# First convolution product of a conformer block: 13 of 16 chunks as two seven-product quads inside the attention passes

## The chip, the cores and the metric

The kernel runs on one core of a Trainium2 chip. The metric is the device time of one execution in microseconds; the times given are medians of several executions. The kernel before has a median of 1873.56 us over 3 runs (1873.33 to 1876.11).

The engines are TensorE (PE in the profile; PEld is its weight load), VectorE (DVE), ScalarE (ACT), GpSimd (POOL) and SyncE (SP), which issues nearly all of the DMAs. TensorE writes to eight PSUM banks, called s0 to s3 and y0 to y3 in the profile (numbers left out: s and y), and numbered 0 to 7 in the code.

## The reference, cut to what matters

A conformer block for 2 sequences of 4000 tokens with 512 features, in bfloat16: half a feed-forward step, attention with one head, a convolution module, another half feed-forward step. The change touches the convolution module's first product, `h @ w_pw1`, with its gate:

```
    x2 = x1 + attn
    h = _layernorm(x2, axis=-1)
    h = h @ w_pw1                      # 512 x 1024
    a = h[..., :D].copy()
    b = h[..., D:].copy()
    h = a * _sigmoid(b)
    ...                                # 3 taps over time, then a normalization over all tokens
    h = _silu(dc) @ w_pw2
    x3 = x2 + h
```

Each token's 512 normalized features give 1024 columns; the first 512 (values) are multiplied by the sigmoid of the last 512 (gates).

## The kernel before

**Chunks and stages.** The 8000 tokens are 16 chunks of 512 (`NCK`), eight to a sequence (`TCB`); the last chunk of a sequence, 7 and 15, has 416 tokens. The program has three stages: the first feed-forward step over all chunks, then 16 attention passes (one for each chunk of queries, `attention`), then the rest of the convolution module and the second feed-forward step.

**A pass.** Pass `g` goes over 32 key tiles (`KT`) in steps `kt` = 0 to 31. In passes 0 and 8 (`plain`), scores are computed tile by tile. In the others they are computed in seven-product quads (`score_quad`): a 2 x 2 block product with 7 block products instead of 8, at the price of sums of blocks on both sides. A quad holds three banks: c, x and h. Products 1 and 2 go to c; product 5 goes to x and is copied aside; ScalarE copies c's first product into h, to which products 6, 7 and 4 are added in turn, with VectorE reading h between them (`plus`). The softmax-weighted values are computed in the same way by pairs of tiles (`pv`, seven products over banks 3 to 6 and 7). The last value products, left-over tiles and row sums of pass `g` are done in steps 0 to 6 of pass `g + 1` (`units_late`); the new pass's value products begin in step 7 (`units`). In between, steps 0 to 6 hold the late products of the pass before, and its output is projected in steps 9 and 13 and normalized for the convolution in steps 9 to 20 (`ln_beside`), by ScalarE, with DMA transposes into `lnT[0]`.

**The convolution's first product.** `pw1` computes one block of 128 output columns with four matmuls of 512 columns. `conv_b` does a gate block and its tanh; `conv_a` does a value block and multiplies it by one plus the tanh (the factor of a half is in the taps' weights). The hook of the passes (`att_hook`) calls `pair(t, jj)`, one `conv_b` and one step later one `conv_a`: block pairs 0 and 1 of chunk `t` in steps 24 and 28 of pass `t + 1`, pairs 2 and 3 in steps 3 and 5 of pass `t + 2`. Three steps after each, `taps_beside` does the three taps of the same column block of chunk `t - 1`: three ScalarE products, two VectorE additions, statistics, and a staging tile that a DMA stores.

**The left-over tile.** 4000 tokens are 31 tiles of 128 and 32 more. `tail_scores` does the scores of those 32 keys in one bank, their exponentials go through DRAM (`pqd`) to another layout (`ptail`), and the value products that use them (`pv_rest`) run late. It stands in step 24 (21 in pass 0).

**What sets the order.** In the first pass over the program each operation is recorded as a node (`Plan`), with a duration from a table of costs and its dependencies; a list scheduler then runs the nodes engine by engine, takes for each engine what is ready and due first, and emits that order. TensorE may draw work up to 8 us ahead of its written order; `S.front` gives score quads an advance. Within an engine the emitted order is fixed: an instruction that waits holds up what is behind it. Because a helper emits everything, nearly all rows of the profile carry its line, L95, and are told apart by tiles: `work`, `wff`, `keys`, `sums` and `xt` are the SBUF regions.

**Memory.** The residual rows of a chunk (`XT`) are stored to DRAM (`put_x`) and loaded again (`get_x`) into slots of the region `xt`; in the passes two slots alternate. `acc`, two tiles of 2 KB, serve the joined value products (`u4`) in turn. `lrow` holds row sums. The convolution's first weights (`Wp1`) are loaded once, in pass 0. In pass 14 VectorE writes 12 diagonal tap matrices (`tap_matrix`) for the last chunks.

Of the kernel before, what the change touches and what calls it, by code (L numbers as in the profile page):

```python
# [17 lines left out]
CHUNK = TPC * TILE  # L18
N = B * T
TCB = -(-T // CHUNK)  # L20
FC = F // 128
NCK = B * TCB
# [7 lines left out]
HC, HD, HF = CHUNK // 2, D // 2, FC // 2  # L30
KT = -(-T // 128)
REST = T % 128
DC = D // 128
# [8 lines left out]
def width(c):  # L42

    return CHUNK if c % TCB < TCB - 1 else T - (TCB - 1) * CHUNK
# [515 lines left out]
class Conformer:  # L560
# [35 lines left out]
    def memory(self):  # L596
# [142 lines left out]
        lrow, self.b_lrow = C.view(oHL, CHUNK, F32, parts=1), C.buf("lrow", oHL, 4 * CHUNK)  # L739
# [4 lines left out]
        self.b_acc = [C.buf("acc", oACC + s * 2048, 4 * CHUNK) for s in range(2)]  # L744
# [4 lines left out]
        self.b_Wp1 = W.buf("Wp1", 0, 8192)  # L749
        self.Wp2 = C.view(oWvo, 2048).rearrange("p (c f) -> p c f", c=DC)  # L750
        self.b_Wp2 = C.buf("Wp2", oWvo, 4096)

# [14 lines left out]
        self.b_asb = [W.buf("asb", 8192 + k * 2048, 4 * CHUNK) for k in range(3)]  # L767
        self.tmp = [W.view(12288 + n * 1024, CHUNK) for n in range(2)]
        self.b_tmp = [W.buf("tmp", 12288 + n * 1024, 2 * CHUNK) for n in range(2)]
        self.bst = W.view(14592, DC * NCK * 6, F32).rearrange("p (c t s) -> p c t s", c=DC, t=NCK)  # L770
        self.b_bst = [W.buf("bst", 14592 + cc * NCK * 24, NCK * 24) for cc in range(DC)]
        gof = [16128, 20240]
# [6 lines left out]
        self.thl = [W.view(24576 + s * 1024, CHUNK) for s in range(4)]  # L779
        self.b_thl = [W.buf("thl", 24576 + s * 1024, 2 * CHUNK) for s in range(4)]  # L780
        self.b_th = [W.buf("th", 24576 + s * 2048, 4 * CHUNK) for s in range(2)]
        self.dwd = [W.view(28672 + i * 256, 128) for i in range(DC * KW)]
        self.b_dwd = [W.buf("dwd", 28672 + i * 256, 256) for i in range(DC * KW)]

# [1091 lines left out]
    def pv_join(self, g, step):  # L1876

        S, W, hw = self.S, width(g), width(g) // 2
        y = lambda n: self.bank(self.PV_BANK[n])
        t2, b_t2 = self.t2[:, 0:W], self.b_t2  # L1880
        half = lambda q, lo: self.OT[:, lo:lo + 2, q * hw:(q + 1) * hw]
        two = lambda ap: ap.rearrange("p (c k) -> p c k", c=2)

        def dve(out, n, x, b_x, writes):
            ps, b_ps = y(n)
            src = ps[:, 0:W]
            if len(out.shape) == 3:
# [3 lines left out]
        s = g % TCB % 2  # L1891
        u4, b_u4 = self.acc[1 - s][:, 0:W], self.b_acc[1 - s]
        if step == 0:
            self.act(t2, y(1)[0][:, 0:W], AF.Copy, [y(1)[1]], [b_t2])
        elif step == 1:
            dve(t2, 6, t2, b_t2, [b_t2])
        elif step == 2:
            dve(u4, 5, t2, b_t2, [b_u4])
        elif step == 3:
            dve(half(1, 2), 7, u4, b_u4, self.b_OTq[1][2:4])  # L1900
        elif step == 4:
            dve(half(0, 2), 3, u4, b_u4, self.b_OTq[0][2:4])
        elif step == 5:
            dve(half(1, 0), 4, t2, b_t2, self.b_OTq[1][0:2])
        else:
            self.act(half(0, 0), two(y(2)[0][:, 0:W]), AF.Copy, [y(2)[1]], self.b_OTq[0][0:2])
# [146 lines left out]

    ASIDE = {3: (5, 7), 4: (5, 7), 5: (5, 7), 6: (5, 7), 16: (0,), 20: (0,)}

    def attention(self, old, hook):
# [238 lines left out]

    def sum_row(self, g, q):

        hw, s = width(g) // 2, g % TCB % 2
        ps, b_ps = self.bank(self.PV_BANK[7 if q else 3])
        u4, b_u4 = self.acc[1 - s], self.b_acc[1 - s]  # L2300
# [73 lines left out]
    def conv_a(self, t, jj, bank=None):  # L2374
# [28 lines left out]
                reads=[b_ps, self.b_th[k]], writes=wr)  # L2403
        self.halo_left(t, jj)
        self.halo_right(t, jj)

    def pw1(self, t, cb, bank=None):
        ps, b_ps = bank or self.sbank()
# [227 lines left out]
    def program(self, any_score):  # L2636
# [104 lines left out]
        def pair(t, jj, bank=None):  # L2741
            self.conv_b(t, jj)
            self.after(1, lambda: self.conv_a(t, jj, bank))
            if t:
                self.after(3, lambda: self.taps_beside(t - 1, jj))

        here, there = ((22, 27), (3, 8)) if any_score else ((24, 28), (3, 5))

        def att_hook(g, kt):
            if g == 0 and kt == 8:  # L2750
                self.load(self.Wp1, i["w_pw1"].rearrange("(c p) f -> p c f", p=128), [self.b_Wp1])
            if kt in here and (0 <= g - 1 < tail or g - 1 == tail and here.index(kt) < self.KEEP):
                pair(g - 1, here.index(kt), self.bank(1) if kt == 24 else None)
            if 0 <= g - 2 < tail and kt in there:
# [22 lines left out]
        if any_score:  # L2777
            self.attention_any(old, att_hook, projected)
            for k in range(DC * KW):
                self.tap_matrix(k)  # L2780
            while self.later:
                self.tick()
            self.act(self.nr1, self.onef, AF.Sigmoid, [self.b_onef], [self.b_nr1])
            self.pop(3)
            self.pop(1)
            self.sums_direct(last % 2)
        else:
            self.ring = [0, 1, 2]
            self.attention(old, att_hook)
            self.attention_end()  # L2790
        self.wa_back()
        self.ring = list(range(4))
# [8 lines left out]
        def gate(eng):  # L2801
            gates.pop(0)(eng)
# [234 lines left out]
```

## Time and profile before

| | |
|---|---|
| median of 3 runs | 1873.56 us (1873.33 to 1876.11) |
| the profiled execution | 1873.41 us |
| its span, first to last instruction | 1869.3 us |
| granted TensorE clock | 0.999 |
| first feed-forward stage | about 0 to 420 us |
| attention passes | about 420 to 1385 us |
| rest of the convolution module | about 1385 to 1450 us |
| second feed-forward stage | about 1450 us to the end |

How to read it: a row of a group names the helper's line, the engine, the operation, output tiles <- input tiles, the shape, and the count; then busy time in us and the mean length of one in ns; then the idle time of the engine just before such instructions and who ended it. Matmuls are pipelined, so the length of one (379 ns for 512 columns) is longer than the interval at which they follow one another; a row in time order that merges several consecutive ones gives start, total length and count, from which the interval follows. A row of a table by stretches gives the stretch, its length, and then the busy time and count for PE, PEld, DVE, ACT and POOL, the granted clock, the DMA share and GB/s.

### The profile page before, as it was taken

To read this page: it belongs to the slowest core of one execution; us is meant where nothing else is said; L and a number is where in the kernel's file an instruction comes from. 1 tells how busy PE (TensorE), PEld (TensorE's weight loads), DVE (VectorE), ACT (ScalarE), POOL (GpSimd) and SP (SyncE) were. 2 spreads that over 40 slices of the span, in tenths; PEclk is the share of its full clock that TensorE was granted. 3 is DMA by queue.
4 is the path that set the end of the run, shared out by engine and by line. 5 is a ranking of instruction groups with operands and counts; after the bars stand their busy time and mean duration, and the time that the engine had idled before them with its cause. 6 is when DMAs were issued, how large, how long until landed. Compare 5 with 4: busy or idle time off the path is not lost.

```text
span 1869.3 us, 39049 instructions
## 1 busy us (share of the span) xinstructions
PE 1850.3 (99%) x15410; PEld 1455.7 (78%) x15524; DVE 1382.7 (74%) x2978; ACT 1323.1 (71%) x2338; POOL 145.2 (8%) x354
## 2 busy tenths in 40 slices
PE   9999999999999999999999999999999999999998
PEld 6888888866777777777677777777775888888887
DVE  8889999767557666665666566656658988888887
ACT  6877777754656776677667666776658787777766
POOL 3000000010000000000000000000011000000000
PEclk9999999999999999999999999999999999999999
DMA  7233344297545555456944444443365222221211
GB/s 200 83 90 91 80 113 106 55 268 212 174 137 148 159 166 157 107 139 160 241 131 135 126 115 107 121 137 115 111 196 169 66 60 77 60 67 45 53 45 56
DMA packets 311971, 227.90 MB, mean 122 GB/s; under 512 B 191123, under 2 KB 282582, under 8 KB 311525
## 3 DMA queue, kind: packets, MB, share of 16 engines
q1 hardware_dynamic: 311252, 225.06, 44.0%
q8 instruction: 124, 2.03, 0.5%
q14 instruction: 67, 0.54, 0.1%
q10 hardware_dynamic: 528, 0.26, 0.0%
HBM read 128.47 MB, written 55.82 MB: 99 GB/s over the span
## 4 chain that ended last, share of the span: by engine, by line
PE 95%; ACT 3%; DVE 1%; issue 1%; DMA 0%; POOL 0%; SPq 0%; DVEq 0%
PE y L95 49%; PE s L95 46%; ACT sums L95 1%; DVE work L95 1%; ACT wff L95 1%; ACT work L95 1%; DVE xt L95 0%; DMA work<-work 0%; DMA xt<-in_x_dram 0%; DVE wff L95 0%; ACT keys L95 0%; DVE keys L95 0%; POOL work L95 0%; ACT s L95 0%; ACT xt L95 0%
## 5 line engine op out<-in xcount | busy, mean ns | idle before, releaser
L95 ACT ACTIVATE sums<-s 128x512 bf16<-128x512 f32 (+4 forms) x505 | 294.8, 586 | 146.0 <-PE s L95 141.7
L95 DVE TENSOR_TENSOR sums<-sums 128x512 bf16<-128x512 bf16 (+3 forms) x528 | 201.8, 400 | 91.7 <-ACT sums L95 80.2
L95 ACT ACTIVATE keys<-s 128x512 bf16<-128x512 f32 (+3 forms) x275 | 157.1, 574 | 136.0 <-PE s L95 113.0
L95 PE MATMUL y<-work,keys 128*128 128x256 bf16 x1920 | 244.4, 273 | 0.0
L95 PE MATMUL s<-work,keys 128*128 128x256 bf16 (+5 forms) x1430 | 220.4, 290 | 1.6 <-issue 0.2
L95 PE MATMUL y<-sums,keys 128*128 128x256 bf16 (+1 forms) x1440 | 214.6, 270 | 0.0
L95 PE MATMUL s<-sums 128*128 128x256 bf16 (+1 forms) x1428 | 212.5, 272 | 0.3 <-DVE s L95 0.3
L95 ACT ACTIVATE work<-xt,work 128x512 bf16<-128x512 bf16 x268 | 203.5, 785 | 9.8 <-DVE work L95 7.7
L95 PE MATMUL y<-wff,keys 128*128 128x256 bf16 (+2 forms) x1590 | 208.9, 276 | 0.2
L95 PEld LDWEIGHTS y<-work,keys 128*128 128x128 bf16 x1920 | 187.6, 98 | 22.7 <-DVE work L95 0.3
L95 PE MATMUL y<-work,wff 128*128 128x256 bf16 (+4 forms) x1188 | 197.6, 289 | 0.8 <-ACT keys L95 0.8
L95 DVE TENSOR_TENSOR keys<-keys 128x1024 bf16<-128x1024 bf16 (+2 forms) x262 | 170.2, 664 | 35.5 <-ACT keys L95 18.3
L95 PEld LDWEIGHTS y<-wff,keys 128*128 128x128 bf16 (+1 forms) x1592 | 151.2, 98 | 30.2 <-issue 3.3
L95 DVE BATCH_NORM_STATS2 work<-xt 128x6 f32<-128x512 bf16 x251 | 163.1, 681 | 2.5 <-DMA xt<-in_x_dram 1.8
L95 PEld LDWEIGHTS s<-work,keys 128*128 128x128 bf16 (+1 forms) x1456 | 117.3, 97 | 56.0 <-ACT sums L95 5.6
L95 PEld LDWEIGHTS y<-sums,keys 128*128 128x128 bf16 x1440 | 137.1, 98 | 27.5 <-issue 6.1
L95 PEld LDWEIGHTS s<-sums 128*128 128x128 bf16 x1428 | 139.0, 98 | 22.7 <-DVE s L95 0.6
L95 POOL TENSOR_TENSOR work<-work 128x4 f32<-128x4 f32 (+3 forms) x107 | 91.8, 860 | 763.1 <-DVE work L95 750.5
L95 PE MATMUL y<-sums,xt 128*128 128x256 bf16 (+1 forms) x960 | 148.3, 270 | 0.0
L95 PEld LDWEIGHTS y<-work,wff 128*128 128x128 bf16 x1188 | 114.8, 98 | 26.6 <-issue 1.5
L95 DVE TENSOR_TENSOR s<-s,xt 128x512 f32<-128x512 f32 (+1 forms) x98 | 67.2, 686 | 85.8 <-ACT work L95 40.1
L95 PE MATMUL s<-xt,keys 128*128 128x256 bf16 (+1 forms) x816 | 124.2, 270 | 0.3 <-DVE xt L95 0.2
(139 smaller groups left out, 3105.3 us busy)
## 6 DMA issues: line engine op xcount, KB each, us to landing
xt<-kfd SPq DMA_DIRECT2D x98, 384.0 KB, 3.4
xt<-v12d SPq DMA_DIRECT2D x105, 256.0 KB, 2.9
xd<-xt SPq DMA_DIRECT2D x28, 512.0 KB, 2.7
xt<-xd SPq DMA_DIRECT2D x28, 512.0 KB, 3.9
out_dram<-xt SPq DMA_DIRECT2D x14, 512.0 KB, 2.9
xt<-in_x_dram SPq DMA_DIRECT2D x13, 512.0 KB, 4.3
dcvd<-wff SPq DMA_DIRECT2D x48, 128.0 KB, 2.0
keys<-dcvd SPq DMA_DIRECT2D x12, 512.0 KB, 3.8
```

What stands on the lines that cost most here:

```text
L95: return getattr(eng, self.name)(*self.args, **self.kw)
```

## The change

For chunks 0 to 6 and 8 to 13 (all but the last chunk of each sequence and chunk 14), `pair` is no longer called. In its place:

- `conv_weights` makes three sums of weight blocks in pass 0 (steps 14 to 18) and, in place, a fourth (step 20). Chunks 7 and 14 need the plain weights: `conv_reload` loads the overwritten quarter again in passes 8 and 15 (step 10), and the in-place difference is made again in pass 9.
- `conv_sums` makes three differences of token blocks of chunk `t` in steps 24 to 26 of pass `t + 1`, in the tiles `ltm`, and one in place in step 27.
- `conv_quad` does two quads for chunk `t` in steps 2 to 7 of pass `t + 2`: quad 0 in banks 7, 5, 3, quad 1 in banks 7, 5, 4. Each gives two blocks of gate columns and two of value columns for the chunk's two halves. `between` calls it after the late value products of a step and before the new ones.
- `taps_beside` of chunk `t - 1` stands in steps 8, 11, 14 and 17.

To make room, `acc` becomes one tile `u4`, which also serves quad 0 as `m5c[0]`; `lrow` moves to the other half of `acc`; the weight sums take the second slot of the residual rows and the old place of `lrow`, so that the passes keep one slot; quad 1's own tiles lie over the taps' temporaries and staging tiles. The tap matrices are written three to a pass in passes 9 to 12. In the last pass `tail_scores` stands in step 16 instead of 24.

The diff, cut to its core:

```
-        self.acc = [C.view(oACC + s * 2048, CHUNK, F32) for s in range(2)]
+        self.u4, self.b_u4 = C.view(oACC, CHUNK, F32), C.buf("u4", oACC, 4 * CHUNK)
+        self.WF = [R.view(o, 2 * D).rearrange("p (j f) -> p j f", j=2) for R, o in ((self.XR, 4096), (self.XR, 6144), (C, oHL))]
...
-                if kt == (24 if g else 21):
+                if kt == (21 if g == 0 else 24 if g < NCK - 1 else 16):
                     self.tail_scores(g)
                 if g:
                     self.units_late(g - 1, kt)
+                between(g, kt)
                 self.units(g, kt)
...
+    def conv_quad(self, t, i, step):
...
+        forms = {1: (part(0, 0), at(0, 0)), 2: (part(0, 1), at(1, 0)), 3: (form(2), at(1, 1)), 4: (part(1, 1), t_form(2)),
+                 5: (form(0), t_form(0)), 6: (form(1), t_form(1)), 7: (part(1, 0), at(0, 1))}
+        def product(n, ps, b_ps, start=False):
+            (a, b_a), (m, b_m) = forms[n]
+            for u in range(2):
+                for j in range(2):
+                    self.mm(ps[:, u * HC:(u + 1) * HC].rearrange("p (t k) -> p t k", t=2), a(u, j), m(j),
+                            start and u == 0 and j == 0, u == 1 and j == 1, [b_a, *b_m], b_ps, skip_group_check=True)
...
+        if step == 0:
+            product(5, x, b_x, True)
+            if width(t + 1) < CHUNK:
+                self.mm(h[:, width(t + 1):], self.WF[0][:, 0, 0:128], self.WF[0][:, 0, 0:CHUNK - width(t + 1)], False, True,
+                        [self.b_WF[0]], b_h, skip_group_check=True)
+            self.act(m5, x[:, :], AF.Copy, [b_x], [b_m5])
+            product(1, c, b_c, True)
+            self.act(h[:, :], c[:, :], AF.Copy, [b_c], [b_h])
+        elif step == 1:
+            product(6, h, b_h)
+            plus(x[:, :], b_x)
+            product(2, c, b_c)
+            tanh(c, b_c, 0)
+        elif step == 2:
+            product(7, h, b_h)
+            plus(m5, b_m5)
+            product(3, x, b_x)
+            tanh(x, b_x, 1)
+            gate(m5, b_m5, 1)
+        else:
+            product(4, h, b_h)
+            gate(h[:, :], b_h, 0)
...
+        def plain(t):
+            return any_score or t == TCB - 1
+        def quads(g, kt):
+            if g == 0 and kt in WEIGHTS:
+                self.conv_weights(WEIGHTS.index(kt))
+            if g == TCB + 1 and kt == 10:
+                self.conv_weights(3)
+            if g - 1 in (TCB - 1, tail) and kt == 10:
+                self.conv_reload()
+            if 0 <= g - 1 < tail and not plain(g - 1) and kt in TOKENS:
+                self.conv_sums(TOKENS.index(kt))
+            t = g - 2
+            if 0 <= t < tail and not plain(t):
+                for n, step in CONV.get(kt, ()):
+                    self.conv_quad(t, n, step)
+                if t and kt in TAPS:
+                    self.taps_beside(t - 1, TAPS.index(kt))
+        WEIGHTS, TOKENS, TAPS = (14, 16, 18, 20), (24, 25, 26, 27), (8, 11, 14, 17)
+        CONV = {2: ((0, 0),), 3: ((0, 1),), 4: ((0, 2),), 5: ((0, 3), (1, 0)), 6: ((1, 1),), 7: ((1, 2), (1, 3))}
...
-                self.get_x(g, self.slot(g, 0, 2))
+                self.get_x(g, self.slot(g, 0, 2 if any_score else 1))
...
-            if g == NCK - 2 and 16 <= kt < 28 and not any_score:
-                self.tap_matrix(kt - 16)
+            if TCB < g <= TCB + DC and kt in (7, 15, 23) and not any_score:
+                self.tap_matrix((g - TCB - 1) * KW + (kt - 7) // 8)
```

In the functions for scores of any size (`any_score`), which are built as a second program and don't run on these inputs, nothing of this applies.

More of the change, by code (lines that the diff above doesn't have):

```diff
@@ L749, in memory @@
         self.b_Wp1 = W.buf("Wp1", 0, 8192)
+        self.WF = [R.view(o, 2 * D).rearrange("p (j f) -> p j f", j=2) for R, o in ((self.XR, 4096), (self.XR, 6144), (C, oHL))]
+        self.b_WF = [R.buf("WF", o, 4 * D) for R, o in ((self.XR, 4096), (self.XR, 6144), (C, oHL))]
         self.Wp2 = C.view(oWvo, 2048).rearrange("p (c f) -> p c f", c=DC)
@@ L781, in memory @@
         self.b_th = [W.buf("th", 24576 + s * 2048, 4 * CHUNK) for s in range(2)]
+        homes = ((24576, 26624), (8192, 10240))
+        self.thc = [[W.view(o, CHUNK, F32) for o in pair] for pair in homes]
+        self.b_thc = [self.b_th, [W.buf("thc", o, 4 * CHUNK) for o in homes[1]]]
         self.dwd = [W.view(28672 + i * 256, 128) for i in range(DC * KW)]
@@ L2054, with attention @@
     ASIDE = {3: (5, 7), 4: (5, 7), 5: (5, 7), 6: (5, 7), 16: (0,), 20: (0,)}
-    def attention(self, old, hook):
+    def attention(self, old, hook, between):
         S = self.S
@@ L2405, in conv_a, with conv_weights @@
         self.halo_right(t, jj)
+    def conv_weights(self, step):
+        a11, a12, a21, a22 = [self.Wp1[:, 2 * k:2 * k + 2, f * D:(f + 1) * D] for f in (1, 0) for k in range(2)]
+        s1, s2, s4 = self.WF
+        b1, b2, b4 = [[b] for b in self.b_WF]
+        out, x, y, op, rd, wr = ((s1, a21, a22, ALU.add, [], b1), (s2, s1, a11, ALU.subtract, b1, b2),
+                                 (s4, a12, s2, ALU.subtract, b2, b4), (a21, a11, a21, ALU.subtract, [], [self.b_Wp1]))[step]
+        self.S.op("DVE", lambda e: e.tensor_tensor(out=out, in0=x, in1=y, op=op), reads=rd + [self.b_Wp1], writes=wr)
@@ new lines, in conv_reload, with conv_tokens, conv_form, conv_sums @@
+    def conv_reload(self):
+        src = self.i["w_pw1"].rearrange("(c p) f -> p c f", p=128)
+        self.load(self.Wp1[:, 0:2, 0:D], src[:, 0:2, 0:D], [self.b_Wp1])
+    def conv_tokens(self, k, h, flat=True):
+        x = self.lnT[0][:, 2 * h:2 * h + 2, 2 * k:2 * k + 2, :]
+        return x.rearrange("p t c k -> p t (c k)") if flat else x
+    def conv_form(self, m):
+        return self.ltm[m].rearrange("p (t c k) -> p t c k", t=2, c=2)
+    def conv_sums(self, step):
+        b = self.conv_tokens
+        t1, t2, t4 = [self.ltm[m].rearrange("p (t n) -> p t n", t=2) for m in range(3)]
+        b1, b2, b4 = [[x] for x in self.b_ltm[0:3]]
+        out, x, y, rd, wr = ((t1, b(0, 1), b(0, 0), [], b1), (t2, b(1, 1), t1, b1, b2), (t4, b(1, 0), t2, b2, b4),
+                             (b(0, 1), b(1, 1), b(0, 1), [], self.b_lnT[0][2:4]))[step]
+        self.S.op("DVE", lambda e: e.tensor_tensor(out=out, in0=x, in1=y, op=ALU.subtract),
+                  reads=rd + self.b_lnT[0], writes=wr)
@@ L2751, in att_hook @@
                 self.load(self.Wp1, i["w_pw1"].rearrange("(c p) f -> p c f", p=128), [self.b_Wp1])
-            if kt in here and (0 <= g - 1 < tail or g - 1 == tail and here.index(kt) < self.KEEP):
+            if kt in here and (0 <= g - 1 < tail and plain(g - 1) or g - 1 == tail and here.index(kt) < self.KEEP):
                 pair(g - 1, here.index(kt), self.bank(1) if kt == 24 else None)
-            if 0 <= g - 2 < tail and kt in there:
+            if 0 <= g - 2 < tail and kt in there and plain(g - 2):
                 pair(g - 2, 2 + there.index(kt))
@@ L2788, in program @@
             self.ring = [0, 1, 2]
-            self.attention(old, att_hook)
+            self.attention(old, att_hook, quads)
             self.attention_end()
```

33 lines of the change are left out of this document (27 added, 6 removed).

## The prediction

> **What bounds the kernel now.** I read the profile's page first, then busy time by stage, then TensorE's waits in the stage that the change rewrites, then the order in time there.
>
> ```profile
> span 1869.3 us, 39049 instructions
> PE 1850.3 (99%) x15410; PEld 1455.7 (78%) x15524; DVE 1382.7 (74%) x2978; ACT 1323.1 (71%) x2338; POOL 145.2 (8%) x354
> PE 95%; ACT 3%; DVE 1%; issue 1%; DMA 0%; POOL 0%; SPq 0%; DVEq 0%
> ```
>
> TensorE is busy for 99% of the span and holds 95% of the chain that ended last. Busy time of pipelined matmuls can hide gaps, so I looked at the stage alone. The attention passes, which carry the convolution product, run from about 420 to 1385 us; the rows give length, then PE, PEld, DVE, ACT and POOL busy time.
>
> ```profile
> 420.00:1385.00 965.00, 959.92 (x7827) 718.52 (x7901) 606.95 (x1375) 649.73 (x1193) 59.26 (x226) 1.00 0.53 147
> 584.00:604.00 20.00, 19.95 (x162) 15.19 (x163) 14.19 (x29) 12.41 (x21) 0.71 (x5) 1.00 0.46 121
> 604.00:624.00 20.00, 19.89 (x162) 15.21 (x162) 11.49 (x29) 14.94 (x29) 2.28 (x6) 1.00 0.63 200
> 624.00:647.10 23.10, 23.00 (x194) 16.91 (x196) 15.82 (x37) 17.05 (x32) 1.19 (x5) 1.00 0.60 164
> ```
>
> The last three rows together are one full pass (63.1 us). VectorE works 41.5 us of it and ScalarE 44.4; TensorE works all of it, at a granted clock of 1.00. And it hardly waits for anybody. These are all of its waits in that stage (us in total, times, longest):
>
> ```profile
> PE s L95 <- ACT s L95: 0.3, 1, 0.3
> PE s L95 <- ACT sums L95: 0.2, 1, 0.2
> PE s L95 <- DVE xt L95: 0.2, 1, 0.2
> PE s L95 <- issue: 0.2, 1, 0.2
> ```
>
> 0.9 us in 965. So the pass is as long as its matmuls take to issue, and a matmul left out is time gained, as long as the others still find their inputs ready.
>
> **The change, part by part.** *The matmuls.* Today a chunk's first convolution product is 32 matmuls of 512 columns (8 column blocks by 4 contraction slices). Two quads make it 2 x 7 products x 4 = 56 of 256. Comparing the orders in which the two programs' instructions stand, 416 matmuls of 512 go (13 x 32), 728 of 256 come (13 x 56) and two of 96 that only clear stale columns of a bank. What one costs in a stream, from runs in time order (start, length, count) and the mean length of one:
>
> ```profile
> 1373.95 1.89 PE L95 MATMUL s<-work,wff 128*128 128x512 bf16 x8
> 1340.46 2.13 PE L95 MATMUL y<-sums,work 128*128 128x256 bf16 x18
> L95 PE MATMUL s<-work,wff 128*128 128x512 bf16 x236 | 60.1, 379 | 0.0
> L95 PE MATMUL y<-sums,work 128*128 128x256 bf16 x420 | 53.2, 273 | 0.0
> ```
>
> A run's length is the issue intervals plus the last one's full length: (1.89 - 0.379) / 7 = 0.2159 us for 512 columns, (2.13 - 0.273) / 17 = 0.1092 us for 256. A chunk goes from 32 x 0.2159 = 6.91 to 56 x 0.1092 = 6.12 us; that is -0.79, and 13 x -0.79 = -10.3 us. The two clearing matmuls are under 0.1 each, so -10.1.
>
> *Half the columns per weight load.* A chunk now loads 56 weight blocks instead of 32. Whether that is free is seen in a score quad of today's kernel, which has the very shape of the new quads:
>
> ```profile
> 605.88 0.60 PE L95 MATMUL s<-xt 128*128 128x256 bf16 x4
> 606.21 0.42 PEld L95 LDWEIGHTS s<-work,keys 128*128 128x128 bf16 x4
> 606.31 0.60 PE L95 MATMUL s<-work,keys 128*128 128x256 bf16 x4
> 606.58 0.70 DVE L95 TENSOR_TENSOR s<-s,xt 128x512 f32<-128x512 f32 x1 [0.26 <-ACT xt L95]
> 606.75 0.82 PE L95 MATMUL y<-sums,keys 128*128 128x256 bf16 x6
> 607.40 0.60 PE L95 MATMUL s<-xt,keys 128*128 128x256 bf16 x4
> L95 PEld LDWEIGHTS s<-work,keys 128*128 128x128 bf16 (+1 forms) x1456 | 117.3, 97 | 56.0 <-ACT sums L95 5.6
> ```
>
> The four loads from 606.21 run while the matmuls from 605.88 and 606.31 do, and the matmul starts stay 0.43 us per four apart. A load of 97 ns fits under the 109 ns of a 256-column matmul. Cost 0; if it were not hidden, 24 x 97 ns = 2.33 us a chunk. [...]
>
> *New waits inside a quad.* The h bank of a quad is added to by products 6, 7 and 4, with a VectorE addition reading it between them. In the same rows, product 6 starts at 605.88, ten other matmuls follow (4 + 6), the addition runs 606.58 to 607.28, and product 7 starts at 607.40, directly behind the ten. So ten matmuls (1.09 us) are just enough cover if VectorE is free. In the changed order the first quad of a chunk has at least 16 such matmuls between (1.75 us), mostly value products of the late pass; the second quad, at the end of the left-over products, has 10 or 12 (1.09 to 1.31 us). Cost if VectorE is free: 0. If an f32 addition lies ahead of it at both places of the second quad: 2 x 0.69. How likely that is I take from what exists: there are 98 score quads (one stream of key forms each) with that dependence, and the stage's waits are 0.9 us.
>
> ```profile
> xt<-kfd SPq DMA_DIRECT2D x98, 384.0 KB, 3.4
> ```
>
> That is 0.01 us a quad, 0.3 us for 26. I take 0.5, because the second quads have the shorter cover, and keep 0 and 13 x 1.38 = 17.9 as ends.
>
> *More work for VectorE and ScalarE.* The prices:
>
> ```profile
> L95 DVE TENSOR_TENSOR s<-s,xt 128x512 f32<-128x512 f32 x84 | 58.7, 699 | 74.4 <-ACT work L95 40.1 <-PE s L95 21.1 <-ACT wff L95 7.9
> L95 DVE TENSOR_TENSOR xt<-s,xt 128x512 f32<-128x512 f32 x84 | 58.1, 691 | 52.5 <-PE s L95 52.4
> L95 DVE TENSOR_TENSOR wff<-wff 128x512 bf16<-128x512 bf16 x96 | 40.1, 418 | 12.0 <-ACT wff L95 10.3
> L95 DVE SCALAR_TENSOR_TENSOR wff<-wff,s 128x512 bf16<-128x512 f32 x29 | 19.9, 687 | 12.1 <-PE s L95 11.8
> L95 DVE BATCH_NORM_STATS2 wff<-wff 128x6 f32<-128x512 bf16 x48 | 33.3, 693 | 1.5
> L95 ACT ACTIVATE s<-s 128x512 f32<-128x512 f32 x84 | 48.9, 582 | 71.6 <-PE s L95 70.1 <-PE y L95 0.6
> ```
>
> A chunk adds four f32 additions (2.8 us) and four token forms (4 x 0.42) on VectorE and four copies (2.3 us) on ScalarE; tanhs and gates stay four each. A pass then has VectorE at 41.5 + 4.5 = 46 and ScalarE at 46.7 of 62.3 us: hidden behind TensorE. In the first 20 us of a pass, where both quads now sit, VectorE has 14.2, gains 2.8 and two gates (1.4), and loses the second pair's taps (per block two additions and the statistics, 2 x 1.53): 15.3 of 20. Tighter, still under TensorE. The five weight forms (1,024 wide, in passes 0 and 9) are at most two bf16 additions each, 0.84 us, in stretches with no consumer near: 0. If no cover were left, VectorE's new work would cost at most its 4.5 us a chunk.
>
> *Moved transfers.* With one slot instead of two for the residual rows, a chunk's load now waits for the store of the chunk before it, and on SP's queue the key and value streams stand behind it.
>
> ```profile
> xd<-xt SPq DMA_DIRECT2D x28, 512.0 KB, 2.7
> xt<-xd SPq DMA_DIRECT2D x28, 512.0 KB, 3.9
> work<-work SPq DMA_TRANSPOSE x174, 2.5
> dcvd<-wff SPq DMA_DIRECT2D x48, 128.0 KB, 2.0
> wff<-in_w_pw_dram SPq DMA_DIRECT2D x1, 1024.0 KB, 7.6
> ```
>
> In the changed order 11 to 20 other SP issues stand between store and load, of 31 to 44 in a pass, so about a third of a pass (20 us) against a landing of 2.7; the rows are wanted 18 steps, some 36 us, later. Cost 0; uncovered, 2.7 us a pass, less the slack of the streams. VectorE's first token form waits for transposes (2.5 us), issued at least 5 us of TensorE's work before; behind it in VectorE's queue stand pair forms that value products need. ScalarE's tanhs of the second quad write where the taps' results were staged, and wait for their stores (2.0 us), issued at least 15 us before. The two reloads of a quarter of the weights take no longer than the whole's 7.6 us and have 14 steps of 2 us. All 0. The tap matrices only change passes.
>
> *Left-over scores sooner.* They now stand eight steps earlier in the last pass. Today:
>
> ```profile
> 1373.28 0.37 PE L95 MATMUL s<-work,keys 128*32 128x104 bf16 x16
> 1383.49 0.25 PE L95 MATMUL y<-xt,keys 128*128 128x208 bf16 x1
> 1383.68 0.26 PE L95 MATMUL y<-wff,keys 32*128 32x208 bf16 x1
> ```
>
> The products that need them start 10.4 us later, 0.19 us behind the matmul before. At most 0.1 to gain: 0.
>
> **Sum.** The profiled execution took 1873.41 us (its span plus 4.1), 0.15 under the median of the runs. 1873.4 - 10.1 + 0.5 = 1863.8. The instructions before the passes and from shortly after them stand in the same order, so those stages keep their time.
>
> **The rivals.** *Half given back.* VectorE is late by one bf16 form (0.42 us) once a chunk: 13 x 0.42 = 5.5, so 1868.8. For it: the second quad's cover is only as long as the chain, and the token and pair forms share VectorE's in-order queue. Against: 15.3 of 20 us.
>
> *Slower: the second quad waits.* At its two places an f32 addition lies ahead of the one that TensorE needs; products 7 and 4 then wait 0.69 us each, and everything behind them, the next pass's value products in the same banks among it, moves. 13 x 1.38 = 17.9 against -10.1 gives 1881.2. It decides from 0.78 us a chunk. For it: the late pass's joins, the row sums and the quad's own two additions all fall there. Against: 98 quads with 0.9 us of waits.
>
> *Nothing gained.* The passes are paced by something beside TensorE and keep 63.1 us: 1873.4. Only the 0.9 us of waits speaks to it, and against it.
>
> *Weight loads show.* 2.33 - 0.79 = +1.54 us a chunk, 1873.4 + 20.0 = 1893.4; the rows at 606 us refute it. [...]
>
> **How the numbers follow.** Forecast 0.81, half given back 0.10, second quad waits 0.05, nothing gained 0.03, loads show 0.01. The likeliest is 1863.8 and its own range 1862.3 to 1866. Reaching to the half-given-back case, the range is 1862 to 1869, which holds about 0.87. About 0.2% (3.7 us) is what a measurement of this kernel can tell from no change, so faster means under 1869.8: 0.81 + 0.10 = 0.91; same 0.03; slower 0.06.
>
> **What would show it.** In the profile after, TensorE has about 312 more matmuls, a full pass lasts about 62.3 us instead of 63.1, TensorE's waits in the passes stay under 2 us, and the weight loads stay under the matmuls. The first step is wrong if a pass shortens by something else with no waits; the second if matmuls on y<-work,wff or y<-work,xt wait for VectorE, the sign of the slower case; the third if SP's streams land late and the value products wait for a DMA. A pass of 63.1 us with idle TensorE would make the whole argument wrong.

## The result, and the profile after

The changed kernel takes 1867.91 us (median of 8 runs, 1866.64 to 1868.96) against 1873.93 us for the kernel before beside it (8 runs): a ratio of 0.9967, 95% interval 0.9956 to 0.9978. That is 6.0 us less where 9.7 were forecast. The profiled execution is the slowest of the eight, 1868.96 us with a span of 1864.0, so 4.96 us lie outside the span (4.11 before). Its page:

```profile
span 1864.0 us, 39949 instructions
PE 1845.8 (99%) x15838; PEld 1488.5 (80%) x15838; DVE 1428.7 (77%) x3087; ACT 1350.1 (72%) x2390; POOL 139.9 (8%) x354
PE 95%; DVE 2%; DMA 1%; ACT 1%; issue 0%; SPq 0%; POOL 0%; DVEq 0%; ACTq 0%
```

TensorE still sets the end. What is new in the chain is VectorE at 2% and DMA at 1%.

**A regular pass.** ScalarE computes one exponential of the form `xt<-s` into bf16 in each pass, which makes a good marker. The rows (start, length, engine) are from the timeline, the kernel before first:

```profile
1139.39 0.60 ACT L95 ACTIVATE xt<-s 128x512 bf16<-128x512 f32 x1 [0.30 <-PE s L95]
1202.49 0.60 ACT L95 ACTIVATE xt<-s 128x512 bf16<-128x512 f32 x1 [0.30 <-PE s L95]
```

and the changed one:

```profile
1130.60 0.60 ACT L95 ACTIVATE xt<-s 128x512 bf16<-128x512 f32 x1 [0.48 <-PE s L95]
1192.88 0.60 ACT L95 ACTIVATE xt<-s 128x512 bf16<-128x512 f32 x1 [0.48 <-PE s L95]
1255.17 0.60 ACT L95 ACTIVATE xt<-s 128x512 bf16<-128x512 f32 x1 [0.48 <-PE s L95]
```

63.10 us a pass became 62.28 and 62.29. The two groups of TensorE that hold most of the quads' h and x products, with the idle time before them in the last column, and a stretch of the timeline with the second quad in it:

```profile
L95 PE MATMUL y<-work,wff 128*128 128x256 bf16 x312 | 46.8, 273 | 0.0
L95 PE MATMUL y<-work,xt 128*128 128x256 bf16 x156 | 23.5, 273 | 0.0
```

```profile
1200.30 0.60 PE L95 MATMUL s<-xt 128*128 128x256 bf16 x4
1200.74 0.60 PE L95 MATMUL y<-work,xt 128*128 128x256 bf16 x4
1201.17 0.60 PE L95 MATMUL s<-work,keys 128*128 128x256 bf16 x4
1201.61 0.60 PE L95 MATMUL y<-work,wff 128*128 128x256 bf16 x4
```

No quad product waits for anything, and four matmuls still start every 0.43 to 0.44 us. So each pass brings what was forecast. The rest is lost elsewhere. TensorE's waits from 420 to 1385 us:

```profile
PE y L95 <- DMA xt<-v12d: 1.1, 1, 1.1
PE s L95 <- ACT sums L95: 1.0, 2, 0.8
PE s L95 <- ACT s L95: 0.3, 1, 0.3
PE s L95 <- DVE xt L95: 0.2, 1, 0.2
```

Two of them are new: the one for the value stream (`xt<-v12d`), in pass 8, and the 0.8 for ScalarE, in the last pass. To place the rest, I take the same instruction in both traces and subtract its start times (changed minus before, profiled executions):

| place (the instruction, its start before and after) | difference, us |
|---|---|
| pass 0: the exponential, 453.58 and 454.20 | +0.61 |
| pass 14: the same, 1328.05 and 1316.78 | -11.27 |
| end of attention: ScalarE's table load, 1381.90 and 1374.17 | -7.73 |
| the next table load, 1412.60 and 1404.88 | -7.72 |
| first output DMA of the second feed-forward step, 1520.30 and 1514.69 | -5.61 |
| end of the span, 1869.3 and 1864.0 | -5.3 |
| whole execution, 1873.41 and 1868.96 | -4.45 |

(The -11.27 holds 3.45 us that are only put off: 16 matmuls of 512 columns that stood at the end of a pass now stand, as quads, in the next.) To the end of attention the sum closes: -10.1, the start's 0.6, the wait of 1.1 in pass 8 and the one of 0.8 in the last pass give -7.6, against -7.73. Then 2.1 us are lost at the start of the second feed-forward step, where both programs have the same TensorE instructions in the same order; 0.3 to the end of the span; and 0.85 outside it.

What VectorE waits for at that start, in the same stretch of both kernels. Before, from 1433 to 1498 us:

```profile
DVE xt L95 <- PE y L95: 2.0, 6, 0.6
...
DVE sums L95 <- DMA work<-work: 1.0, 3, 0.5
```

and after, from 1425 to 1490:

```profile
DVE sums L95 <- DMA work<-work: 3.6, 2, 2.0
DVE xt L95 <- PE y L95: 2.0, 6, 0.6
```

The wait for the DMA transposes (`work<-work`) has grown by 2.6 us; the one for TensorE (`PE y`) is as it was. There are two places. VectorE's first addition behind the first group of four transposes is shown further below (its wait grows from 0.54 to 1.58 us). The first one behind the second group, some 30 us later, in the kernel before and in the changed one:

```profile
1470.39 0.42 DVE L95 TENSOR_TENSOR sums<-work 128x512 bf16<-128x512 bf16 x1 [0.25 <-DMA work<-work]
```

```profile
1465.44 0.42 DVE L95 TENSOR_TENSOR sums<-work 128x512 bf16<-128x512 bf16 x1 [1.97 <-DMA work<-work]
```

Compared instruction by instruction from the table load on, TensorE falls 1.05 us behind at the first group and 1.1 more at the second.

### The profile page after: what moved, and what is told of

Its sections match the earlier page's. It is cut to its first block, busy times and chain, and to the rows that moved or that the text cites. A ratio compares the mean times of both kernels' runs of the same rounds, so it can differ in the third digit from the quotient of the medians.

```text
span 1864.0 us, 39949 instructions
## 1 busy us (share of the span) xinstructions
PE 1845.8 (99%) x15838; PEld 1488.5 (80%) x15838; DVE 1428.7 (77%) x3087; ACT 1350.1 (72%) x2390; POOL 139.9 (8%) x354
## 4 chain that ended last, share of the span: by engine, by line
PE 95%; DVE 2%; DMA 1%; ACT 1%; issue 0%; SPq 0%; POOL 0%; DVEq 0%; ACTq 0%
PE y L95 50%; PE s L95 45%; DVE work L95 1%; ACT work L95 0%; DMA work<-work 0%; DMA wff<-in_w_ff_a_dram 0%; DVE sums L95 0%; DMA xt<-v12d 0%; DVE xt L95 0%; DVE keys L95 0%; ACT keys L95 0%; ACT sums L95 0%; SPq L95 0%; DVE wff L95 0%; DVE s L95 0%
## 5 line engine op out<-in xcount | busy, mean ns | idle before, releaser
L95 PE MATMUL s<-work,keys 128*128 128x256 bf16 (+5 forms) x1456 | 225.1, 292 | 0.2 <-ACT sums L95 0.2
L95 PE MATMUL y<-wff,keys 128*128 128x256 bf16 (+3 forms) x1592 | 209.3, 276 | 0.2 <-DVE keys L95 0.2
L95 PE MATMUL y<-sums,keys 128*128 128x256 bf16 (+1 forms) x1440 | 205.3, 270 | 0.0
L95 PE MATMUL y<-work,wff 128*128 128x256 bf16 (+3 forms) x1308 | 195.2, 272 | 0.9 <-ACT keys L95 0.8
L95 PEld LDWEIGHTS y<-work,wff 128*128 128x128 bf16 x1308 | 126.0, 98 | 18.4 <-issue 1.5
L95 PE MATMUL s<-work 128*128 128x512 bf16 (+4 forms) x545 | 131.6, 375 | 2.0 <-DVE work L95 1.7
```

The costliest lines, as they stand in the source:

```text
L95: return getattr(eng, self.name)(*self.args, **self.kw)
```

## The experiments

**Is it one of the two kernels' executions, the quads, or the rest of the change?** Four kernels beside 25 runs of the kernel before. The first two are the changed kernel and the kernel before, again.

> The changed kernel once more, for a second trace. Theory: each of the 13 chunks brings its 0.79 us, and the rest of the 10.2 us is lost at single places outside the quads (pass 8, the last pass, the start of the second feed-forward stage, the start of the program). Then 1866.5 to 1869 us, a regular pass of 62.2 to 62.4 us (63.1 before); waits set by the order (pass 8, last pass) come again at the same places, and waits that come from a DMA's landing (second feed-forward stage, program start) differ by 0.5 us or more. Rival, every quad gives back 0.3 us: a regular pass of 62.6 us or more.

> The kernel before once more, for a second trace. Theory: 1873 to 1874.5 us, regular passes of 63.1 us, TensorE's waits in the passes under 1.5 us; the first transposes of the second feed-forward stage may land as late as in the changed kernel (up to 2 us of waits there), which would make that loss no part of the change. If they land early again, the loss belongs to the change.

Measured: 1867.7 us for the changed kernel (ratio 0.9966, 0.9954 to 0.9979), 1873.2 for the kernel before (1.0, 0.9991 to 1.0009), whose transposes landed early again. The profiled execution of the changed one again lost in the last pass (0.8 us of wait) and at the second feed-forward step (3.0 between the table load and the first output, with a drop of TensorE's clock in it that is told below), and waited 0.6 in pass 8 where the first had 1.1; it started only 0.14 us later than before.

The third has no quads and all the rest:

```
         def plain(t):
-            return any_score or t == TCB - 1
+            return True
         def quads(g, kt):
-            (weight forms and reloads)
```

> Everything of the change but the quads: one slot for the residual rows, one joined tile, tap matrices in passes 9 to 12, left-over scores of the last pass sooner; the convolution product as before, by blocks. Theory: these cost nothing in common passes, 1873 to 1875 us. Rival, the rest of the change costs the 4 us that are missing: 1877 to 1878.5 us.

Measured: 1875.2 us, ratio 1.0011 (1.0002 to 1.002). Moved slots, moved tap matrices and sooner scores cost about 1.4 us together by the medians (0.4 to 3.7 by the interval), and none of it at the second feed-forward step, where this kernel loses 0.01. TensorE's waits show the part in the last pass:

```profile
PE s L95 <- ACT sums L95: 0.7, 2, 0.4
```

The fourth has the quads, and the last left-over scores where they were:

```
-                if kt == (21 if g == 0 else 24 if g < NCK - 1 else 16):
+                if kt == (21 if g == 0 else 24):
```

> The changed kernel with the last pass's left-over scores in step 24 again. Theory: the move gained nothing, and the wait of 1.0 us in the last pass may be its price: 1866.5 to 1868.5 us. Rival, the move is worth something: 1869 us or more, with a wait at the left-over value products at the end of the passes.

Measured: 1868.54 us (0.9969, 0.9958 to 0.9979), 0.8 more than the changed kernel beside it, with intervals that overlap. The profiled execution is by far the slowest of its eight (1873.72 us; the other seven took 1866.66 to 1869.28), and TensorE's clock drops twice in it. In it the wait of 0.8 us for ScalarE is gone, but TensorE then waits for VectorE at the end of attention, and for the value stream more often:

```profile
PE y L95 <- DMA xt<-v12d: 2.0, 3, 0.7
PE s L95 <- DVE xt L95: 0.6, 2, 0.4
PE s L95 <- DVE work L95: 0.4, 1, 0.4
```

In this execution 1.9 us of the lead go between the last exponential and the end of attention, where the changed kernel loses 0.9. That the move pays for itself is likely by this, but not shown.

**Why the second feed-forward step?** The DMA records have packets of the kind "instruction": of 16 KB on one queue (q8), and of 8 KB on another (q14). They are called code packets here. Before, then after:

```profile
q8 instruction: 124, 2.03, 0.5%
q14 instruction: 67, 0.54, 0.1%
```

```profile
q8 instruction: 126, 2.06, 0.5%
q14 instruction: 70, 0.57, 0.1%
```

Counted out, the first queue's packets follow TensorE: there is about one for each 256 of its instructions (between the starts of two packets stand 256 weight loads and matmuls in the median, in both kernels; by that count, an estimate, 64 bytes each). The records have 31,260 of these before and 31,833 after (weight loads, as many matmuls, and a few others). TensorE itself is not seen to wait for them: in the traces of the two kernels nearly every idle time of TensorE over 0.15 us ends with work of another engine or a DMA; the one that does not is 0.16 us long, in the kernel before. But each packet takes about 1.1 us in the DMA records, where the transposes' packets stand too (both are counted in shares of the same 16 DMA engines: 0.5% for q8, 44.0% for q1, which has the transposes, in the kernel before). 573 instructions more are two packets and 61 instructions, so from then on every packet stands elsewhere against the transfers (at the first group 4.85 us behind the first transpose, where it was 8.46). In the changed kernel one starts while the last transpose of the first group is under way, and another in the last one of the second group. For the first group, the view of DMAs from 1433 to 1435 us, and then, for the kernel before, that of 1440 to 1441 (the last transpose alone):

```profile
q8 instruction: 1, 0.02, 3.5%
issues: line engine op xcount, KB each, median us to landing
xt<-xd SPq DMA_DIRECT2D x1, 512.0 KB, 3.9
work<-work SPq DMA_TRANSPOSE x1, 3.5
```

```profile
work<-work SPq DMA_TRANSPOSE x1, 2.5
```

VectorE's first addition behind the transposes, the kernel before and the changed one:

```profile
1442.65 0.43 DVE L95 TENSOR_TENSOR sums<-work 128x512 bf16<-128x512 bf16 x1 [0.54 <-DMA work<-work]
```

```profile
1435.98 0.43 DVE L95 TENSOR_TENSOR sums<-work 128x512 bf16<-128x512 bf16 x1 [1.58 <-DMA work<-work]
```

To test this I change only the number of TensorE instructions, in the warm-up at the start, whose product nobody reads: some of its wide matmuls become narrow ones (about 28 ns each), and more narrow ones are added (here 106 in the place of 9: 97 more). All other instructions stand in the same order.

```
             self.mm(ps[:, 0:CHUNK], self.zero[:, 0:128], self.zero, True, True, ...)
+        if self.S.plan:
+            emit = self.S.plan.pe[-1].emit
+            emit[3:-1] = [lambda: self.S.eng["PE"].matmul(ps[0:32, 0:16],
+                self.zero[:, 0:32], self.zero[:, 0:16], start=True, stop=True)] * 106
```

Three kernels: 97 and 128 more on the changed kernel, 31 more on the kernel before.

> The changed kernel with 97 more TensorE matmuls in its warm-up (nine of the thirteen wide ones there become narrow, and 97 narrow ones are added: 32 rows by 16 columns on a buffer of zeros; nothing else moves). In the records a 16 KB packet of the kind 'instruction' comes once for every 256 TensorE matmuls and weight loads and takes about 1.1 us. The change added 573 TensorE instructions in all, which is two such packets and 61 instructions; at the start of the second feed-forward stage its packets come about 3.6 us earlier against the transposes, between the last transpose and the load behind it. 97 pairs are 194 instructions and put that back to 255 of 256. Theory C (code packets delay transfers): the first VectorE addition of that stage is back at about 6.5 us after the first transpose (7.6 and 8.2 in the changed kernel), the stage gives back its 2.1 to 2.9 us, and the time is 1865 to 1866 against the changed kernel's 1867.8. Theory D (the loss there comes from the data: what the passes leave in the queues): nothing changes there, 1867 to 1869. The 0.85 us more that lie outside the span: C with the end of the program in it, back to 4.1; otherwise 4.9 stays. The warm-up may cost or save up to 0.7 us by itself.

> The control: 128 more matmuls in the warm-up instead of 97. 256 instructions are one whole 16 KB packet, so all later packets keep their place against the transfers. Theory C: second feed-forward stage as in the changed kernel (first addition 7.5 to 8.2 us behind the first transpose, 2 to 3 us lost), time 1867 to 1869. Theory D says the same of this run. If it too gets faster, the gain of the run with 97 comes from the warm-up and not from the packets' place.

> The kernel before with 31 more matmuls in its warm-up: 62 instructions, which puts its code packets where the changed kernel has them. Theory C: it loses 1 to 3 us at the start of the second feed-forward stage with no quad in it, and comes out at 1875 to 1877. Theory D: 1873.2 to 1874, no change. Time outside the span: 4.9 by the packets, 4.0 otherwise.

Measured: 1867.98 us with 97 (ratio 0.9971, 0.996 to 0.9983), 1868.14 with 128 (0.9972, 0.9961 to 0.9982), and 1876.79 for the kernel before with 31 (1.002, 1.0011 to 1.0029). The places came out as the packets say: with 97 the second feed-forward step loses 0.03 us, with 128 it loses 2.8 (1.3 of it by the clock, below), and the kernel before, with no quad in it, now loses 1.5 there. Its first addition:

```profile
1446.06 0.43 DVE L95 TENSOR_TENSOR sums<-work 128x512 bf16<-128x512 bf16 x1 [2.00 <-DMA work<-work]
```

But the total with 97 did not get better as expected: TensorE waits in the passes instead (the first in pass 8, the others in the last pass; that its packets now fall among those transfers is the author's estimate):

```profile
PE y L95 <- DMA wff<-pqd: 0.9, 1, 0.9
PE y L95 <- DMA xt<-v12d: 0.5, 1, 0.5
PE s L95 <- DMA work<-work: 0.5, 1, 0.5
```

**Can the packets be placed better, and do the quads alone bring 0.8 a pass?** Two more numbers of added matmuls, 110 and 113 (the latter with five wide matmuls behind the narrow ones), the scores at step 20 on top of 110, and quads in the second half's six chunks only:

```
         def plain(t):
-            return any_score or t == TCB - 1
+            return any_score or t < TCB
...
-            if g == 0 and kt in WEIGHTS:
+            if g == 0 and kt in WEIGHTS[:3]:
...
-            if g - 1 in (TCB - 1, tail) and kt == 10:
+            if g - 1 == tail and kt == 10:
```

> The changed kernel with 110 more narrow matmuls in its warm-up: 220 instructions, so a code packet comes about 2.1 us later against the transfers than in the changed kernel, and 1.5 us earlier than with 97. Theory C (each place loses time only where a code packet falls into a row of transfers that something waits for): the packet at the second feed-forward stage's start comes about 7 us behind the first transpose, past the load that it delayed, so the first addition is back at 6.5 us and that stage loses nothing; in the last pass it comes at about 1364, before the four loads of wff<-pqd, which cost the run with 97 its gain (waits of 0.9 and 0.5 us), so the 1.4 us there do not appear. Time 1865 to 1866.5. If the places do not decide: 1867.5 to 1868.5, as the three before it.

> The same, and the left-over scores of the last pass at step 20 instead of 16 (24 before the change). Of the last pass the changed kernel loses about 0.9 us, 0.8 of it in one wait of TensorE for ScalarE on a tile of 'sums' behind the moved scores; with the scores at 24 the end of attention lost 1.9 instead. If the wait comes from the scores' place: at 20 it is shorter and nothing new waits at the end of attention, 0.5 to 0.9 us less than the run beside it. If any place costs the same: no difference, within 0.3.

> Quads only in the six chunks of the second half (8 to 13); the first seven are computed as before the change, and the weights need no reload between. 265 more TensorE instructions than before: a whole code packet and 9, so the packets stand as in the kernel before. Theory T and C together: each of the six passes is 0.8 us shorter, 4.7 in all; the second feed-forward stage loses nothing; the last pass loses its 0.8 to 0.9; there is no chunk with quads in flight at the middle, so no wait for the value stream there. Span 1865.3 to 1866 against 1869.3. Time outside the span 4.1 if it comes from how many quads there are, 4.9 if from their being there: 1869.4 to 1870.9. Rival (the loss belongs to the quads, 4 us over 13): 6 x 0.46 = 2.8 us off, span 1866.5 or more, with no wait missing in the middle.

Measured: 1868.13 us with 110 (0.9968, 0.9956 to 0.998), 1870.4 with the scores at 20 (0.9977, 0.9968 to 0.9987), 1871.54 with quads in six chunks (0.9988, 0.9978 to 0.9997). With 110 the addition is back at 6.5 us behind the first transpose, as expected, but 1.3 us are lost in that step all the same: the view by windows shows TensorE's granted clock (third column from the end) at little more than half for about 4 us.

```profile
1416.00:1418.00 2.00, 0.99 (x8) 0.55 (x8) 1.97 (x6) 1.61 (x4) 0.40 (x1) 1.00 1.18 301
1418.00:1420.00 2.00, 1.50 (x12) 1.29 (x12) 1.66 (x4) 1.25 (x3) 0.00 (x0) 0.59 1.11 348
1420.00:1422.00 2.00, 2.00 (x11) 1.37 (x10) 1.90 (x5) 2.00 (x5) 0.00 (x0) 0.56 0.97 347
```

And the warm-up itself cost 1.5 us. The scores at step 20 were a miss: 2.3 us worse than the run beside it, with the waits for VectorE of the run with the old place back, and, as in that run, a drop of the clock right behind the end of attention, from 1384 us. The drops seem to be most of the miss: the five of its ten runs with a granted clock of 0.998 took 1870.56 to 1871.40, the other five 1866.78 to 1870.25.

```profile
1384.00:1386.00 2.00, 2.00 (x15) 1.76 (x13) 0.00 (x0) 0.00 (x0) 0.00 (x0) 0.50 0.00 0
```

The six-chunk kernel loses 0.01 us at the second feed-forward step: 265 more instructions are a whole packet and 9, and its packets stand as before the change. Outside the span it has 4.08 us (median of 11). Of the five intervals between the exponentials of passes 9 to 14, four shorten by 0.68 to 0.81 us and the first by 0.19. Its span of 1867.4 (median) is more than I expected, though: the last pass waits for two DMAs as well as for ScalarE.

```profile
PE s L95 <- ACT sums L95: 1.0, 2, 0.8
PE s L95 <- DMA work<-work: 0.4, 1, 0.4
...
PE y L95 <- DMA xt<-v12d: 0.2, 1, 0.2
```

By its total alone it would fit the rival; its passes and its second feed-forward step speak for the theory, and 0.5 to 0.8 us of what it lacks is not placed.

> A try for a faster version: the changed kernel with 113 more narrow matmuls in its warm-up, and five wide ones behind them instead of one, because the start took 0.9 to 1.5 us longer in the runs with 110 and 128. 226 instructions put the code packet 1.8 us later against the transfers than in the changed kernel. Theory C: the second feed-forward stage loses nothing (first addition 6.5 us behind the first transpose), the last pass waits 0.4 us for a DMA at most beside the 0.8 for ScalarE, and with a start as in the changed kernel it is 1.5 us faster than that: 1866.0 to 1866.8. If the start still costs 1 us or the places give back elsewhere what they bring here: 1867.3 to 1868.2.

> For the 0.85 us that all runs with quads in 13 chunks have outside their span, and those with none or with 6 have not: the kernel before with 287 more narrow matmuls in the warm-up, 574 instructions, as many as the change adds to TensorE's program. If TensorE's program length makes it, 4.9 lies outside the span; if it is something else of the change (the other engines' programs, the work itself), 4.1. Its packets stand as in the changed kernel, so theory C says again that the second feed-forward stage loses 1.4 to 2 us with no quad in it. The start is longer by some 5 us (296 narrow matmuls at 28 ns are 8.3 us, where 3 were), which says nothing.

Measured: 1869.11 us with 113 (1865.48 to 1870.49, ratio 0.9969, 0.9958 to 0.9981), no better than the changed kernel; two of its seven runs, at 1865.5, are the shortest seen. Its packet came at 6.36 us, and the addition at 8.52. The kernel before with 287 more takes 1882.99 (1.0048, 1.0033 to 1.0064), most of it the long warm-up, in which TensorE stands idle for 1.65 us between narrow matmuls with nobody named (what for was not shown); its second feed-forward step loses 2.7, and 3.85 to 4.25 us lie outside its span.

The records of fourteen profiled executions at the start of the second feed-forward step, in us behind its first transpose (the last transpose is issued at 3.9 and lands, undisturbed, at 6.4):

| kernel | 16 KB packet at | first addition at |
|---|---|---|
| before, 287 more | 4.80 | 8.01 |
| changed, scores as before | 4.84 | 7.88 |
| changed | 4.85 | 7.56 |
| changed, 128 more | 4.89 | 7.94 |
| before, 31 more | 4.90 | 7.97 |
| changed, again | 5.59 | 8.19 |
| changed, 113 more | 6.36 | 8.52 |
| changed, 110 more, scores at 20 | 6.56 | 6.53 |
| changed, 110 more | 7.08 | 6.53 |
| before, again | 8.31 | 6.51 |
| no quads, rest of the change | 8.34 | 6.51 |
| changed, 97 more | 8.35 | 6.53 |
| quads in six chunks | 8.43 | 6.52 |
| before | 8.46 | 6.52 |

Whether there are quads plays no part; where the packet falls does. The step from late to on time lies between 6.36 and 6.56, where the last transpose lands. The second group repeats it: only in the changed kernel and in the kernel before with 287 more does a packet start while that group's last transpose is under way, and there it lands after 4.25 and 4.31 us, in the other twelve after 2.50 to 2.53. So the 2.1 us of the changed kernel and the 2.7 of the kernel with 287 more are two such delays each.

## Why the prediction was right, and where it was not

The time fell into the range of 1862 to 1869, but not into the forecast's own, 1862.3 to 1866. It lies where the range had been widened for the case "half given back", and that case's cause, a VectorE that is late once a chunk, did not occur. So the gain in the passes was understood, and that the range holds the total was luck. Point by point:

- *The matmuls, -10.1.* Right: 0.81 to 0.82 us a pass where 0.79 was worked out.
- *Weight loads, 0.* Right: 80% of the span is weight load now, and four quad products still start every 0.43 us.
- *Waits inside a quad, 0.5.* None is seen; nor is the late form of VectorE that was to give half back. Cover of ten to twelve matmuls was enough.
- *More work for VectorE and ScalarE, 0.* Right in the passes: 43.2 and 46.3 us of 62.28.
- *Moved transfers, 0.* Right but for one place: the wait of 1.09 us for the value stream in pass 8. There a code packet starts 2.1 us behind the issue of that stream, and a transpose then keeps SP's queue 2.60 us, where the one before it took 1.2:

```profile
870.27 0.58 SPq L95 DMA_DIRECT2D xt<-v12d  x1
870.90 1.19 SPq L95 DMA_TRANSPOSE keys<-keysd  x1
872.18 2.60 SPq L95 DMA_TRANSPOSE work<-work  x1
```

```profile
875.94 0.53 PE L95 MATMUL y<-sums,xt 128*128 128x208 bf16 x4 [1.09 <-DMA xt<-v12d]
```

  The packet seems to decide here too, in all eight traces with 13 chunks of quads: with the changed kernel again, the scores as before and 128 more it comes 1.7 to 1.8 us behind that issue, and TensorE waits 0.6 to 0.8 us for the stream; with 110, 113 and 97 more and with the scores at 20 it comes 3.3 to 4.6 behind, and there is no wait for the stream in that place. The order of the transfers around it is the same in all eight.
- *Left-over scores sooner, 0.* Mis-sized in both directions: sooner costs a wait of 0.8 us for ScalarE (0.4 without quads), and with the quads in, not moving them took 0.8 more still in the median (1868.54 against 1867.7, which the intervals do not tell apart).
- *"The instructions before the passes and from shortly after them stand in the same order, so those stages keep their time."* This is the step that failed, and the largest part of what is missing: same order, but 2.1 us lost where two code packets fall into transposes (1.5 to 2.7 in the executions with a packet there and an undisturbed clock). The kernel before loses 1.5 and 2.7 with 31 and 287 idle matmuls more. It is no cost of the quads' work, but of the 573 instructions that they add.
- *4.1 us added to the span.* The changed kernel has 0.85 more there: 4.63 to 5.45 in 60 runs with quads in 13 chunks, 3.77 to 4.40 in 125 runs of all others. It is not the length of TensorE's program (287 more matmuls left it at 4.1). What it is stays open.

Together, for the two profiled executions: -10.1 + 0.6 (start) + 1.1 (pass 8) + 0.8 (last pass) + 2.1 (second feed-forward step) + 0.3 (end) + 0.85 (outside) = -4.35, where they differ by 4.45. The changed one is the slowest of its eight; its median is 1.05 lower, that of the kernel before 0.5 higher than the profiled one, which makes the 6.0. The start differs from execution to execution (-0.5 to +1.0 against the first profile, with the warm-up as it was) and was not followed up.

## What to carry to other kernels

In this kernel the code packets behind an edit that added instructions to TensorE stood elsewhere against the transfers, unless the number added was close to a multiple of 256. The 573 of the change moved the packet at the second feed-forward step from 8.46 to 4.85 us behind the first transpose; 256 on top of them (128 matmuls and their loads) left it at 4.89, and the 265 of the six chunks at 8.43. So stages that the edit does not touch kept their order but not their time (2.1 us lost). No other engine and no other kernel was tried. Before believing that an edit costs something at a far place, change only the number of instructions (idle ones in the warm-up) on both kernels and see whether the loss goes and comes. And differences of one or two microseconds between versions of this kernel are partly luck of that placing; a place found for one transfer can spoil another (with 97 more the first addition is back at 6.53 us, but TensorE waits 0.9, 0.5 and 0.5 us in the passes).

## What the runs showed of the hardware

- A 16 KB code packet takes about 1.1 us (0.9 to 1.5 for most). A last transpose of a group that lands after 2.5 us undisturbed took 3.5 to 4.5 us when such a packet started while it was under way. The kernel's own load behind the first group took 3.9 to 4.5 us beside such a packet, against 3.7 in the kernel before.
- In five of the profiled executions TensorE's granted clock fell to 0.50 for about 3.4 us in the midst of the program (the changed kernel again, scores as before, 128 more, 110 more without and with the scores at 20). All five have such a drop at the place of the following rows, behind 3.4 us in which TensorE works 1.8 to 1.9; the two with later scores also have one at 1384 us, behind 10 us of which TensorE works 9.6. So half idleness is not what all drops have in common. The longest single idle time is 0.78 us, and the same gaps, to 0.01 us, stand in executions in which the clock was 1.00 there, as in the kernel before, whose rows these are:

```profile
1416.93 3.06 PE L95 MATMUL y<-work 128*128 128x512 bf16 x12 [0.74 <-ACT work L95]
...
1424.06 0.60 PE L95 MATMUL s<-work,wff 128*128 128x256 bf16 x4 [0.78 <-ACT work L95]
1425.19 0.62 PE L95 MATMUL s<-work 128*128 128x128 bf16 x8 [0.53 <-DVE work L95]
```

  The drop comes and goes between executions of one kernel: the changed kernel has none in its first profiled execution and one in its second. All five executions are of kernels with 13 chunks of quads (five of eight profiled, none of six others). But the drops are not theirs alone, it seems: the five have a mean clock of 0.998 or less and the other nine 0.999 or more, and 0.998 or less stands on record for 17 of the 60 runs with 13 chunks of quads and for 4 of the 125 others. Why was not settled. One such drop costs 1.3 us (the run with 110).
